# Joining the second half of one mLSTM cell visit with the first half of the next in one block of the schedule

## The chip, the cores and the metric

The kernel runs on one core of a Trainium2 chip. The metric is the device time of one execution in microseconds. Several engines work side by side: TensorE (PE, matrix products; its weight loads are listed as PEld), VectorE (DVE), ScalarE (ACT), GpSimd (POOL) and SyncE (SP), which issues nearly all DMA transfers. Each engine works through its own queue in order; semaphores hold an instruction back until what it reads is there and what it overwrites is no longer needed.

## The reference

Two layers. An mLSTM cell runs over a sequence of 768 tokens for 4 batches and 8 heads of width 40; its output, 3072 tokens by 320, goes through a feed-forward layer of width 2048 with a leaky ReLU.

```python
for t in range(S):                                   # q, k, v, o_gate: (4, 8, 768, 40)
    m_new = np.maximum(f_gate[:, :, t] + m, i_gate[:, :, t])
    f_stab = np.exp(f_gate[:, :, t] + m - m_new)
    i_stab = np.exp(i_gate[:, :, t] - m_new)
    m = m_new
    C = f_stab * C + i_stab * einsum('bhd,bhe->bhde', vt, kt)   # state, 40 x 40 a head
    n = f_stab * n + i_stab * kt
    h_tilde = einsum('bhde,bhe->bhd', C, qt)
    nq = einsum('bhd,bhd->bh', n, qt)
    y[:, :, t] = sigmoid(o_gate[:, :, t]) * h_tilde / np.maximum(np.abs(nq), 1.0)

x = y.transpose(0, 2, 1, 3).reshape(3072, 320)
h = x @ w_in                                          # 320 x 2048
out = np.maximum(0.01 * h, h) @ w_out                 # 2048 x 320
```

## The kernel before

**Steps and groups.** The sequence is cut into 6 chunks of 128 tokens. A *step* `s` is one chunk `c = s // 4` of one batch `b = s % 4`, so there are 24 steps; the state of a batch is carried from step `s - 4` to step `s`. A *group* `g` is the feed-forward work on the four steps of chunk `g`. While PE works on the feed-forward of one group, the cells of later chunks are slipped into its stream. The cells of chunks 2 to 5 (steps 8 to 23) lie in groups 1 to 3.

**Units.** The feed-forward of groups 1 to 3 is cut into 30 units a group, numbered on from 0 to 89. Units 0 to 15 of a group are eight pairs: the first half of a pair opens two PSUM banks `ph` and makes 12 matmuls (line 909), the second half makes 8 more, after which ACT applies the leaky ReLU (line 917) and frees the banks. Units 16 to 29 are the second layer, seven products p1, p2, p6, p7, p4, p5, p3 for two token blocks each (`fast_units`; line 984, 16 matmuls, one bank `po` each). It is a scheme with seven products for eight, whose operands are sums that DVE makes: `mix_early` (line 971, in units 8 and 10 of the group, read by p7), line 1002 (read by p5), line 1007 (in p1 of the second block, read by p6) and line 1019 (in p6, read by p3). The products are taken out of PSUM by ACT for p1, p6, p7 and p4, by DVE for p2, p5 and p3.

**Cells.** A step has two halves on PE. The first half, `u_parts(s)`, makes 16 score products (line 652) and the two state updates dC of the sub-blocks of 64 tokens (line 657) into two banks `sd`; DVE then forms the weights `mixed(s)` (line 662) and adds dC of the first sub-block to the state (`state_add(s, 0)`, line 634). The second half, `u_mix(s)`, multiplies weights and states with the values (`pT`, line 745), forms the next state (`state_next(s, 1)` on POOL, line 630, and `state_add(s, 1)` on DVE, line 634), and lets DVE and POOL turn, gate and scale the result (lines 752 to 763), which goes to DRAM and comes back as `xT` of its group. A *visit* is a pair of steps: 8 visits for 16 steps. `u_mix` of a step comes after its `u_parts`, one to five units later.

**Preparation.** `ready(s)` stands some units ahead of a visit: two DVE transposes of k and q (line 537), the product of q with its decay (line 543), then on POOL the first state product (line 630), the placing of v (line 391), line 510 and the mask (line 482); the exponentials on ACT (line 490) follow three units later, three to a unit (`exps`), and what is left of them runs at the head of `u_parts`. `gates(c)` (DVE scans), `gates_exp(c)` (ACT) and `gates_T(c)` (PE transposes `tg`, DVE copies) make the gates of a chunk. `feed(s)` and `load_late` issue the loads of a step, `spread` and `spread_q` the broadcasts of its decays from the DRAM tensor `a_dr`.

**Buffers.** Two PSUM pools of four banks each: `psf` (tag "mm") holds `ph` and `po`; `psc` (tag "c") holds what belongs to the cells (`sd`, `pT`, `tg`). The bank of dC stays taken until `state_add(s, 1)` in `u_mix`. The tile `w` has 128 x 1024 values a step: its first half is the buffer of the exponentials, its second half first takes v as loaded (320 values).

**Order.** The order on PE, DVE, ACT and POOL is that of the program, written out by hand: `plan[unit]` lists what follows each unit. VISITS says after which units `u_parts` of the eight visits stand, MIXES the same for `u_mix`, READY for `ready` of the next visit's two steps, GATES for `gates` and `gates_exp`, UG for `gates_T`. SP's queue is ordered by the planner of the language.

Of the kernel before, what the change touches and what calls it, by code (L numbers as in the profile page):

```python
# [22 lines left out]
def kernel(  # L23
# [314 lines left out]
            nc.tensor.matmul(t[:], lhsT=ident[:], rhs=ident[:], start=True, stop=True)  # L338

    def gates_T(c, bu):  # L340
        tg = psc.tile([P, 5, BH], F32, name="tg", tag="c")
        kinds = 3 if c == 1 else 2
        for n in range(kinds):
            nc.tensor.transpose(tg[:, n, :], bu[:, n, :], ident[:BH, :BH])
        gT[c] = wk.tile([P, 3, BH], F32, name="gT")
        if c > 0:
            for u in range(2):
                last = SL * (u + 1) - 1
                nc.tensor.matmul(  # L349
                    tg[:, 3 + u, :], lhsT=bu[:, 2, last : last + 1].to_broadcast([BH, P]), rhs=ident[:BH, :BH],  # L350
                    start=True, stop=True,
                )
            gL[c] = f0[:, ts(c % 2, 2 * BH)].rearrange("p (u n) -> p u n", u=2)
        nc.vector.tensor_copy(gT[c][:, :kinds], tg[:, :kinds, :])
        if c > 0:
            nc.vector.tensor_copy(gL[c], tg[:, 3:, :])
# [3 lines left out]
    def load(s):  # L360
        c, b = divmod(s, B)
        rows = ts(c, P)
        d = st.setdefault(s, {})
        n = s % NL
        d.update(k=kn[:, n], q=qn[:, n])
        if c == 0:
            d["va"] = S_t[n][:, 1]
            parts = [(d["k"][:, :, :D], k), (d["q"][:, :, :D], q), (d["va"][:, :, :D], v)]
            for dst, src in parts:
                nc.sync.dma_start(dst, src[b, :, rows, :].rearrange("h p d -> p h d"))  # L370
            return
        nc.sync.dma_start(d["k"][:, :, :D], k[b, :, rows, :].rearrange("h p d -> p h d"))
        w = cw.tile([P, H, P], F32, name="w", bufs=NL)
        flat = w[:].rearrange("p h t -> p (h t)")
        d["w"] = flat[:, : H * SL].rearrange("p (h t) -> p h t", t=SL)
        if c == 1:
            for u in range(2):
                for i in range(2):
                    nc.sync.dma_start(
                        S_v[n][ts(u, SL), u, :, i, :DB],  # L380
                        v[b, :, c * P + u * SL : c * P + (u + 1) * SL, DB * i : DB * (i + 1)].rearrange("h p d -> p h d"),
                    )
            return
        d["vn"] = flat[:, H * SL : H * (SL + D)].rearrange("p (h d) -> p h d", d=D)
        nc.sync.dma_start(d["vn"], v[b, :, rows, :].rearrange("h p d -> p h d"))
# [146 lines left out]
    def prep_kq(s):  # L532

        d = st[s]
        d["kqT"] = cw.tile([P, 2, PR * P], F32, name="kqT")
        for i in range(2):
            nc.vector.transpose(
                d["kqT"][:, i].rearrange("p (h t n) -> p h n t", n=TS, t=QW),
                raw_blocks(s, i, QW).rearrange("p (h n) d -> p h n d", n=TS),
            )  # L540
        for r in range(2):
            rows = ts(r, SL)
            nc.vector.tensor_tensor(  # L543
                mixed(s)[rows, 1 - r], d["kqT"][rows, 1].rearrange("p (h t) -> p h t", t=SL), d["ea"][rows], op=ALU.mult,
            )
# [86 lines left out]
    def state_add(s, u):  # L632
        _, new = state_of(s, 1 - u)
        nc.vector.tensor_tensor(new, new, st[s]["dC", u], op=ALU.add)

    def u_parts(s):
        c, b = divmod(s, B)
        d = st[s]
        kqT, w = d["kqT"], d["w"]
        if c == 1:  # L640
            split_qs(s)
        run(lazy.pop(s))
        bank = [psc.tile([P, H, SL], F32, name=f"sd{r}", tag="c") for r in range(2)]
        ends = 2 if c + 1 < NB else 1
        dC = {}
        for u in range(ends):
            flat = bank[u][SL * u : SL * u + D].rearrange("p h t -> p (h t)")[:, : H * 2 * V1]
            dC[u] = flat.rearrange("p (h k d) -> p h k d", k=2, d=V1)
            d["dC", u] = dC[u]
        for h in range(H):  # L650
            for u, toks, rows in subs(s):
                nc.tensor.matmul(  # L652
                    bank[1 - u][toks, h, :], lhsT=kqT[rows, 0, ts(h, SL)], rhs=kqT[rows, 1, ts(h, SL)], start=True, stop=True,
                )
            for u, toks, rows in subs(s):
                if u < ends:
                    nc.tensor.matmul(  # L657
                        dC[u][:, h].rearrange("p k d -> p (k d)"), lhsT=d["ku"][toks, h],
                        rhs=S_v[s % NL][toks, u, h, :, :V1], start=True, stop=True,
                    )  # L660
        for u, toks, rows in subs(s):
            nc.vector.tensor_tensor(mixed(s)[toks, u], w[toks], bank[1 - u][toks], op=ALU.mult)  # L662
        state_add(s, 0)

    def denominators(den, n):

# [67 lines left out]
    def u_mix(s):  # L734

        c, b = divmod(s, B)
        d = st[s]
        prep_o(s)
        pT = psc.tile([P, PR * P], F32, name="pT", tag="c")
        S, m = S_t[s % NL], mixed(s)  # L740
        for u in range(2):
            for j in range(PR):
                for r in range(2):
                    h = 2 * j + r
                    nc.tensor.matmul(  # L745
                        pT[DP * r : DP * (r + 1), j * P + u * SL : j * P + (u + 1) * SL], lhsT=S[:, u, h, :],
                        rhs=m[:, u, h, :], start=True, stop=True,
                    )
        if c + 1 < NB:
            state_next(s, 1)  # L750
        hb = late_t[:, 2, :].rearrange("p (n d) -> p n d", d=QW)
        nc.vector.transpose(hb.rearrange("p (j n) d -> p j n d", n=TB), in_blocks(pT[:]))
        den = cw.tile([P, PR * TB], F32, name="den")
        denominators(den[:], hb[:, :, DB])
        x3 = xb[:, :, :DB]
        nc.vector.scalar_tensor_tensor(  # L756
            x3, in0=raw_blocks(s, 2, DB), scalar=1.0, in1=hb[:, :, :DB], op0=ALU.add, op1=ALU.mult,
        )
        nc.gpsimd.tensor_tensor(x3, x3, den[:].unsqueeze(2).to_broadcast([P, PR * TB, DB]), op=ALU.mult)  # L759
        if c + 1 < NB:  # L760
            state_add(s, 1)
        xq = cw.tile([P, PR * P], F32, name="x")
        nc.vector.transpose(in_blocks(xq[:]), xb[:].rearrange("p (j n) d -> p j n d", n=TB))  # L763
        nc.sync.dma_start(x_dr[s].rearrange("(j p) t -> p j t", p=P), xq[:].rearrange("p (j t) -> p j t", t=P))
        del st[s]
# [302 lines left out]
    def ahead(s):  # L1068

        if s < NS:  # L1070
# [5 lines left out]
            if s < 2 * B:  # L1076
                prep_qs(s)
            else:
                prep_kq(s)
            if s + NR < NS:  # L1080
                load_late(s + NR, 0)
                load_late(s + NR, 1)
# [74 lines left out]
    with tc.manual_schedule(engines={E.PE, E.DVE, E.Activation, E.Pool}):  # L1157
# [46 lines left out]
                    if s + NL < NS:  # L1204
                        feed(s + NL)

        VISITS = (5, 14, 27, 35, 46, 58, 67, 76)
        MIXES = (7, 17, 29, 37, 51, 60, 69, 77)
        READY = ((7, 8), (18, 25), (32, 33), (41, 42), (51, 54), (62, 66), (69, 72))
        GATES = ((1, 4), (20, 25), (38, 44))  # L1210
        UG = (18, 37, 62)
        PER = NF + 14
        SPLIT = (82, 83, 84, 85, 86, 87, 90, 91, 93, 96, 99, 102)
        plan = collections.defaultdict(list)
# [2 lines left out]
            plan[unit].append((fn, args))  # L1217

        def visit_steps(p):
            return (2 * B + 2 * p, 2 * B + 2 * p + 1) if p < len(VISITS) else ()  # L1220

        def gather():

# [5 lines left out]
            mixed_steps.append(s)  # L1229
            gather()  # L1230

        def load_kq(s):
            load_late(s, 0)
            load_late(s, 1)
            spread_q(s)

        def ready(s):
            late[s] = 3
            lazy[s] = prep_exp(s)
            prep_kq(s)  # L1240
            if s + NR < NS:
                load_kq(s + NR)
            state_next(s, 0)
            place_v(s)
            prep_vu(s)
            prep_mask(s)

        mixed_steps = []
        for p, unit in enumerate(VISITS):
            c = 2 + p // 2  # L1250
            if p % 2 == 0 and c + 1 < NB:
                at_unit(GATES[p // 2][0], gates, c + 1)
                at_unit(GATES[p // 2][1], gates_exp, c + 1)
            for s in visit_steps(p):
                at_unit(unit, u_parts, s)
            for s in visit_steps(p + 2):
                at_unit(unit, feed, s)
            for s in visit_steps(p):
                at_unit(MIXES[p], mix, s)
            for s in visit_steps(p + 1):  # L1260
                at_unit(MIXES[p], load_late, s, 2)
            if p % 2 == 1 and c + 1 < NB:
                at_unit(UG[p // 2], u_gates, c + 1)
            for n, s in enumerate(visit_steps(p + 1)):
                at_unit(READY[p][n], ready, s)

# [14 lines left out]
        for g in range(1, NB):  # L1281
# [3 lines left out]
            for i in range(len(ffs)):  # L1285
# [6 lines left out]
                for fn, args in plan[unit]:  # L1292
                    fn(*args)
                gather()
                if unit == MIXES[-1]:
                    open_parts()
                    for n in range(QN):
                        fetch_w_part(n)
# [36 lines left out]
```

## Time and profile before

| | |
|---|---|
| median of 3 runs | 486.96 us (486.33 to 487.30) |
| profiled execution, own time | 486.61 us |
| profiled execution, span from first to last instruction | 484.5 us |
| granted TensorE clock | 1.000 |
| PE busy | 478.6 us, 99% |
| DVE busy | 364.6 us, 75% |
| ACT busy | 196.1 us, 40% |
| POOL busy | 159.4 us, 33% |

Busy times are sums over instructions; matmuls are pipelined, so a busy PE is not a PE at its peak. Groups 1 to 3 lie between about 131 and 364 us of the span. The chain of work that ended last is followed back from the last instruction; each line of it has the start, the length, and the engine, tile, line and count of a run of instructions. A line of the timeline has the start and length in us, the engine, line, operation, what is written and read, shapes, the count, and in brackets the idle time ahead of it with the instruction that ended it.

### The profile page before, as it was taken

The page shows a single profiled execution, that of the slowest core. Times are in us where ns is not written, and L with a number is a line of the kernel's source. Part 1 is how long each engine was busy: PE and PEld are TensorE (multiplying, and loading weights), DVE is VectorE, ACT ScalarE, POOL GpSimd, SP SyncE. Part 2 cuts the span into 40 slices and gives each one's busy share as a digit, 9 for nine tenths or more (in the row PEclk, how much of TensorE's full clock was granted, in tenths as well). Part 3 has the DMA queues.
Part 4 walks back from the last instruction along what each step waited for, and adds up shares of the span by engine and source line. Part 5 has one row for each costly group of instructions (what it writes and reads, how often), then busy time and mean ns, then how long its engine had stood idle before and what let it go on. Part 6 is the DMA issues. An engine that isn't in the chain of part 4 may idle for free.

```text
span 484.5 us, 12804 instructions
## 1 busy us (share of the span) xinstructions
PE 478.6 (99%) x5113; PEld 371.8 (77%) x5113; DVE 364.6 (75%) x601; ACT 196.1 (40%) x499; POOL 159.4 (33%) x207
## 2 busy tenths in 40 slices
PE   8999999999999999999999999999999999999997
PEld 7998655777645489965569985548998899988996
DVE  4689999889917999777887968689899967335611
ACT  2587864743831331405251121524025642156310
POOL 4128024461601826545451645453210002000020
PEclk9999999999999999999999999999999999999999
DMA  7878778896655677667887867774151030100001
GB/s 144 172 164 195 172 163 169 260 211 146 141 129 111 150 144 212 137 158 194 148 193 171 191 149 177 184 183 123 54 225 40 1 108 1 49 8 0 1 1 54
DMA packets 142698, 63.40 MB, mean 131 GB/s; under 512 B 110832, under 2 KB 130864, under 8 KB 142640
## 3 DMA queue, kind: packets, MB, share of 16 engines
q1 hardware_dynamic: 142256, 62.47, 54.4%
q8 instruction: 40, 0.66, 0.6%
q10 hardware_dynamic: 384, 0.13, 0.1%
q14 instruction: 18, 0.15, 0.1%
HBM read 51.68 MB, written 8.27 MB: 124 GB/s over the span
## 4 chain that ended last, share of the span: by engine, by line
PE 95%; DVE 1%; issue 0%; POOL 0%; POOLq 0%; DVEq 0%
PE po L984 32%; PE ph L909 29%; PE ph L835 8%; PE po L945 7%; PE pe L835 4%; PE pT L745 3%; PE sd L652 3%; PE warm L338 2%; PE pa L675 1%; PE sd L657 1%; PE hN L715 1%; PE tk L566 1%; PE tq L552 1%; PE sc L595 1%; PE tkq L580 0%; PE tg L349 0%
## 5 line engine op out<-in xcount | busy, mean ns | idle before, releaser
L909 PE MATMUL ph<-xT,w_in 64*128 64x512 f32 (+1 forms) x680 | 142.3, 569 | 0.0
L909 PEld LDWEIGHTS ph<-xT,w_in 64*128 64x128 f32 x680 | 64.5, 187 | 66.1 <-issue 63.7
L984 PE MATMUL po<-w_out,acts 128*128 128x160 f32 x640 | 91.0, 301 | 0.0
L984 PEld LDWEIGHTS po<-w_out,acts 128*128 128x128 f32 x640 | 87.5, 190 | 3.4 <-ACT w L490 1.5
L917 ACT ACTIVATE acts<-ph 128x512 f32<-128x512 f32 (+1 forms) x68 | 35.1, 567 | 80.3 <-PE ph L909 80.1
L490 ACT ACTIVATE w<-w,gT 128x64 f32<-128x64 f32 (+1 forms) x192 | 51.8, 348 | 28.1 <-POOL w L482 28.1
L630 POOL TENSOR_TENSOR S<-S,f 40x336 f32<-40x336 f32 x36 | 33.9, 941 | 81.2 <-PE pT L745 47.3
L984 PE MATMUL po<-raw,acts 128*128 128x160 f32 x320 | 45.1, 299 | 0.0
L984 PEld LDWEIGHTS po<-raw,acts 128*128 128x128 f32 x320 | 44.0, 190 | 0.0
L1017 POOL TENSOR_TENSOR y<-y,raw 128x160 f32<-128x160 f32 x10 | 5.5, 556 | 112.2 <-ACT y L1016 112.2
L662 DVE TENSOR_TENSOR qn<-w,sd 64x512 f32<-64x512 f32 x40 | 27.4, 684 | 19.9 <-PE sd L657 11.9
L945 PE MATMUL po<-w_out,acts 128*128 128x320 f32 x128 | 36.6, 437 | 0.0
L482 POOL TENSOR_TENSOR w<-w,i 128x512 f32<-128x512 f32 x20 | 32.4, 1618 | 11.7 <-DMA w<-a_dr 11.7
L857 DVE SCALAR_TENSOR_TENSOR acts<-ph,acts 128x512 f32<-128x512 f32 x32 | 20.6, 685 | 20.6 <-ACT acts L855 20.6
L543 DVE TENSOR_TENSOR qn<-kqT,late 64x512 f32<-64x512 f32 x32 | 33.6, 1049 | 1.0
L945 PEld LDWEIGHTS po<-w_out,acts 128*128 128x128 f32 x128 | 23.6, 190 | 9.1
L759 POOL TENSOR_TENSOR xb<-xb,den 128x320 f32<-128x320 f32 x16 | 11.7, 728 | 48.6 <-DVE xb L756 48.6
L855 ACT ACTIVATE acts<-pe 128x512 f32<-128x512 f32 x32 | 17.4, 595 | 19.0 <-PE pe L835 18.9
L763 DVE STREAM_TRANSPOSE x<-xb 128x512 f32<-128x512 f32 x16 | 17.8, 1109 | 7.8 <-POOL xb L759 7.8
L861 ACT ACTIVATE acts<-acts 128x512 f32<-128x512 f32 x32 | 19.7, 633 | 8.1 <-DVE acts L857 8.1
L984 PE MATMUL po<-raw 128*128 128x160 f32 x160 | 22.7, 300 | 0.0
L652 PEld LDWEIGHTS sd<-kqT 40*64 40x64 f32 x640 | 19.6, 135 | 3.7 <-issue 3.7
(166 smaller groups left out, 786.1 us busy)
## 6 DMA issues: line engine op xcount, KB each, us to landing
w<-a_dr SPq DMA_DIRECT2D x40, 128.0 KB, 3.7
rb<-in_k_dram SPq DMA_DIRECT2D x64, 80.0 KB, 2.8
rb<-in_q_dram SPq DMA_DIRECT2D x64, 80.0 KB, 2.6
rb<-in_o_gate_dram SPq DMA_DIRECT2D x64, 80.0 KB, 2.8
xT<-x_dr SPq DMA_DIRECT2D x32, 160.0 KB, 3.1
late<-a_dr SPq DMA_DIRECT2D x32, 128.0 KB, 3.2
x_dr<-x SPq DMA_DIRECT2D x16, 256.0 KB, 3.0
kn<-in_k_dram SPq DMA_DIRECT2D x24, 160.0 KB, 3.4
```

The source lines that it names most:

```text
L482: nc.gpsimd.tensor_tensor(w, w, cm2.unsqueeze(1).to_broadcast([P, H, SL]), op=ALU.add)
L490: yield nc.scalar.activation(w[:, h, :], w[:, h, :], AF.Exp, bias=gT[c][:, 0, bh : bh + 1], scale=1.0)
L543: nc.vector.tensor_tensor(mixed(s)[rows, 1 - r], d["kqT"][rows, 1].rearrange("p (h t) -> p h t", t=SL), d["ea"][rows], op=ALU.mult,)
L630: nc.gpsimd.tensor_tensor(new, old, g, op=ALU.mult)
L652: nc.tensor.matmul(bank[1 - u][toks, h, :], lhsT=kqT[rows, 0, ts(h, SL)], rhs=kqT[rows, 1, ts(h, SL)], start=True, stop=True,)
L662: nc.vector.tensor_tensor(mixed(s)[toks, u], w[toks], bank[1 - u][toks], op=ALU.mult)
L835: nc.tensor.matmul(ph[r][:], lhsT=parts["w", key][n][part, at : at + P], rhs=xs[key][part, slot, :], start=start and slot == 0, stop=stop ...
L857: nc.vector.scalar_tensor_tensor(fs[r], in0=ph[r][:], scalar=1.0 + EPS, in1=fs[r], op0=ALU.mult, op1=ALU.add,)
L909: nc.tensor.matmul(ph[r][:, cols], lhsT=w_row(r, slot, j), rhs=xT[DP * r : DP * (r + 1), slot, bs, :], start=(slot == 0), stop=(slot == KC ...
L917: nc.scalar.activation(acts[:, f, cols], ph[r][:, cols], AF.Prelu, alpha=0.01)
L945: nc.tensor.matmul(po[n][:], lhsT=acts[:, f, ts(n, P)], rhs=w_out[:, f, :], start=(f == 0), stop=(f == NF - 1),)
L984: nc.tensor.matmul(bank[:], lhsT=left[:, f, :], rhs=right[:, f, :], start=f == 0, stop=f == KH - 1)
```

## The change

Instead of 8 visits and 8 mixes at units of their own, there are nine blocks, BLOCKS. Block `p` holds `u_mix` of visit `p - 1`, then `u_parts` of visit `p`; the first has no `u_mix`, the last no `u_parts`. `gates_T` moves into blocks 1, 3 and 5, at their head.

Because `u_mix` of one visit and `u_parts` of the next stand together, the four banks of `psc` go to `sd` alone: `pT`, and `tg` of chunks 3 to 5, move to `psf`. The bank of dC must be free before the next block: the carried state is therefore formed in `u_parts` already (`carry`: a POOL product and a DVE add) in the second half of the tile `w`, where v is no longer needed, and `u_mix` only copies it into place on POOL. The product of q with its decay moves out of `ready` into the block (`scaled`), since its target is still read by the `u_mix` before; `spread_q` of the next step goes with it. `feed` loads for the next visit, where it loaded for the one after it. READY and GATES have other units.

```diff
     def gates_T(c, bu):
-        tg = psc.tile([P, 5, BH], F32, name="tg", tag="c")
+        pool, tag = (psf, "mm") if c > 2 else (psc, "c")
+        tg = pool.tile([P, 5, BH], F32, name="tg", tag=tag)
...
+    def carried(s):
+        w = st[s]["flat"]
+        rows = state_of(s, 0)[0]
+        return w[rows, H * SL : H * SL + H * 2 * V1].rearrange("p (h k d) -> p h k d", k=2, d=V1)
+
+    def carry(s):
+        c, b = divmod(s, B)
+        rows, old = state_of(s, 1)
+        g = gL[c][rows, 1, ts(b, H)].unsqueeze(2).unsqueeze(3).to_broadcast([D, H, 2, V1])
+        nc.gpsimd.tensor_tensor(carried(s), old, g, op=ALU.mult)
+        nc.vector.tensor_tensor(carried(s), carried(s), st[s]["dC", 1], op=ALU.add)
...
         state_add(s, 0)
+        if 1 < c < NB - 1:
+            carry(s)
...
-        pT = psc.tile([P, PR * P], F32, name="pT", tag="c")
+        pT = psf.tile([P, PR * P], F32, name="pT", tag="mm")
...
         if c + 1 < NB:
-            state_next(s, 1)
+            nc.gpsimd.tensor_copy(state_of(s, 0)[1], carried(s))
...
-        if c + 1 < NB:
-            state_add(s, 1)
...
-        VISITS = (5, 14, 27, 35, 46, 58, 67, 76)
-        MIXES = (7, 17, 29, 37, 51, 60, 69, 77)
-        READY = ((7, 8), (18, 25), (32, 33), (41, 42), (51, 54), (62, 66), (69, 72))
-        GATES = ((1, 4), (20, 25), (38, 44))
-        UG = (18, 37, 62)
+        BLOCKS = (2, 8, 19, 29, 39, 51, 61, 71, 78)
+        READY = ((4, 5), (15, 18), (25, 25), (33, 38), (44, 47), (55, 58), (66, 70))
+        GATES = ((3, 4), (20, 28), (36, 47))
+        UG = (1, 3, 5)
...
         def ready(s):
             late[s] = 3
             lazy[s] = prep_exp(s)
             prep_kq(s)
             if s + NR < NS:
-                load_kq(s + NR)
+                load_late(s + NR, 0)
+                load_late(s + NR, 1)
             state_next(s, 0)
...
+        def scaled(s):
+            q_scaled(s)
+            if s + NR < NS:
+                spread_q(s + NR)
...
+            if p in UG:
+                at_unit(unit, u_gates, 3 + UG.index(p))
+            for s in visit_steps(p - 1):
+                at_unit(unit, mix, s)
+            if p:
+                for s in visit_steps(p):
+                    at_unit(unit, scaled, s)
             for s in visit_steps(p):
                 at_unit(unit, u_parts, s)
-            for s in visit_steps(p + 2):
-                at_unit(unit, feed, s)
+            for s in visit_steps(p + 1):
+                at_unit(unit, feed, s) if p else None
             for s in visit_steps(p):
-                at_unit(MIXES[p], mix, s)
-            for s in visit_steps(p + 1):
-                at_unit(MIXES[p], load_late, s, 2)
-            if p % 2 == 1 and c + 1 < NB:
-                at_unit(UG[p // 2], u_gates, c + 1)
+                at_unit(unit, load_late, s, 2) if p else None
             for n, s in enumerate(visit_steps(p + 1)):
                 at_unit(READY[p][n], ready, s)
```

`q_scaled` is the last loop of the old `prep_kq`, now a function of its own.

More of the change, by code (lines that the diff above doesn't have):

```diff
@@ L373, in load @@
         w = cw.tile([P, H, P], F32, name="w", bufs=NL)
-        flat = w[:].rearrange("p h t -> p (h t)")
+        flat = d["flat"] = w[:].rearrange("p h t -> p (h t)")
         d["w"] = flat[:, : H * SL].rearrange("p (h t) -> p h t", t=SL)
@@ L540, in prep_kq, with q_scaled @@
             )
+    def q_scaled(s):
+        d = st[s]
         for r in range(2):
@@ L1219, in visit_steps @@
         def visit_steps(p):
-            return (2 * B + 2 * p, 2 * B + 2 * p + 1) if p < len(VISITS) else ()
+            return (2 * B + 2 * p, 2 * B + 2 * p + 1) if 0 <= p < len(BLOCKS) - 1 else ()
         def gather():
@@ L1230, in mix @@
             gather()
[L1232 to L1235, printed above, removed]
         def ready(s):
@@ L1246, in ready @@
             prep_mask(s)
+        def scaled(s):
+            q_scaled(s)
+            if s + NR < NS:
+                spread_q(s + NR)
         mixed_steps = []
-        for p, unit in enumerate(VISITS):
+        for p, unit in enumerate(BLOCKS):
             c = 2 + p // 2
@@ L1294 @@
                 gather()
-                if unit == MIXES[-1]:
+                if unit == BLOCKS[-1]:
                     open_parts()
```

## The prediction

> **What bounds the kernel now.** I read the page first (parts 1 and 4), then the chain of waits in order of time, then the timelines of VectorE (DVE) and GpSimd (POOL).
>
> ```profile
> PE 478.6 (99%) x5113; PEld 371.8 (77%) x5113; DVE 364.6 (75%) x601; ACT 196.1 (40%) x499; POOL 159.4 (33%) x207
> ...
> PEclk9999999999999999999999999999999999999999
> ...
> PE 95%; DVE 1%; issue 0%; POOL 0%; POOLq 0%; DVEq 0%
> ```
>
> TensorE (PE) is busy for 99% of the span at full clock and is 95% of the chain; from 43 us on the list of waits gives it no wait at all. So time can be won only by shortening PE's own stream, and is lost by any wait put into it. The chain shows what the stream pays where it changes its kind of matmul (start, length, count):
>
> ```profile
> 46.03 1.03 PE tk L566 x64
> ...
> 64.89 1.06 PE hN L715 x32
> 65.95 1.03 PE tk L566 x64
> ...
> 115.34 1.06 PE hN L715 x32
> ...
> 145.93 4.49 PE ph L909 x20
> 150.42 2.02 PE pT L745 x64
> 152.44 15.65 PE ph L909 x72
> ...
> 178.57 2.37 PE po L984 x16
> ...
> 181.63 19.76 PE po L984 x144
> ...
> 229.54 2.02 PE pT L745 x64
> 231.55 0.24 PE tg L344 x2
> ```
>
> Two stretches of ph: (15.65 - 4.49) / (72 - 20) = 0.2146 us a matmul, so 20 of them are 4.29 and the stretch has 0.20 us besides. Two of po: (19.76 - 2.37) / 128 = 0.1359, and 2.37 - 16 x 0.1359 = 0.20 again. Every uninterrupted stretch of feed-forward matmuls thus carries a fixed 0.197 us. A small cell's stretch has a fixed part too, but keeps it whatever stands next to it: pT is 2.02 ahead of ph and ahead of tg, hN 1.06 ahead of tk and of po, tk 1.03 behind ph and behind hN.
>
> **The change, part by part.** PE: before, 16 cell stretches and two tg apart from them (units 18 and 62) break the feed-forward stream 18 times; after, 9 blocks do. 9 x 0.197 = **1.77 us less**. Order inside a block is tg, pT, pT, sd, sd. The trace has no pT followed by sd. Bounds: hN (128*64 tiles) followed by tk (64*40) keeps both at full length, saving nothing more; tq followed by sd at 52.4, both on 64-row tiles, runs on without a break, which would save sd's fixed part of 0.15 (2.01 less 32 groups of 0.058) in 7 blocks, 1.0 more. pT uses 128*64 tiles and sd 40*64 and 64*40, as hN and tk do, so I take nothing. The Trainium skill's page TensorEngine Tiling (Array Packing), Key Properties, says that a change of tiling mode drains the engine; by that rule too the sum stays at 1.77, and the trace agrees where shapes change (0.2 us).
>
> DVE, the engine that PE will wait for. Its timeline at one mix, and one ready step where POOL works beside it:
>
> ```profile
> 151.55 0.72 DVE L752 STREAM_TRANSPOSE late<-pT 128x512 f32<-128x512 f32 x1 [2.63 <-PE pT L745]
> ...
> 153.00 0.49 DVE L756 SCALAR_TENSOR_TENSOR xb<-rb,late 128x320 f32<-128x320 f32 x1
> 153.53 0.51 DVE L634 TENSOR_TENSOR S<-S,sd 40x336 f32<-40x336 f32 x1
> 154.40 1.10 DVE L763 STREAM_TRANSPOSE x<-xb 128x512 f32<-128x512 f32 x1 [0.36 <-POOL xb L759]
> 155.53 0.72 DVE L752 STREAM_TRANSPOSE late<-pT 128x512 f32<-128x512 f32 x1
> ```
>
> The state_add that leaves u_mix (0.51) lay beside POOL's product L759 (153.64 to 154.37), for which L763 waits anyhow: removing it gains nothing. carry() puts its like into u_parts, where nothing covers it: POOL starts 0.15 after its releaser, as L759 does after 153.49; its product costs 0.76 (L630 alone); DVE starts 0.03 later; then the add, 0.50. That is **1.44 us of DVE time a step**, for 12 steps, queued ahead of the next u_parts, mix_early (L971), the ready steps' transposes and the sums L1002 to L1019 that PE reads. POOL's state_next(s,1), 0.76, becomes a copy, 0.45 (L391): off the path. The moved q_scaled (L543, two a step) costs 0.69 each alone (187.89) and 1.05 on average beside POOL's mask; in the block POOL is mostly idle, so I take 0.72. One block on DVE: 2 x 3.98 (mix, 151.55 to 155.53) + 4 x 0.72 + 2 x (1.84 + 1.44) (145.17 to 147.01 for u_parts) = **17.4 us**, or 18.7 with 1.05.
>
> Where PE meets that, from a block's first pT (whose end lets DVE start at 1.1; 2.02 + 2.01 of cells on PE):
> - Block 8, banks: all pT now share psf with ph, which holds two banks there. Unit 10 comes at 0.68 (tg) + 4.03 + 0.2 + 1.72 = 6.6; the second pT's bank is free at 0.68 + 1.1 + 3.98 + 0.75 = 6.5. Slack 0.1; cost 0 to 0.5.
> - End of group 1: p3's second half (unit 29) needs the second L1019. PE is there at 4.2 + 9 x 2.17 = 23.7. DVE: 1.1 + 17.4 + 1.14 + gates(4) + 1.14; gates takes 1.7 alone (133.18) and 3.3 beside POOL (191.04), I take 2.5 as POOL has ready(14) in hand by then: 23.3, no wait. Block 29 opens with tg, which now needs a psf bank, and all four hold p5 and p3 results that DVE releases behind two pairs of transposes (2.6) and 0.5 of adds: 26.4 against PE's 25.9. Wait **0.5**, between 0 and 1.4.
> - Group 2: p6 at unit 50 needs the first L1007. PE is there at 4.2 + 12.9 (three pairs) + 8.7 = 25.8 after block 39; DVE at 1.1 + 17.4 + 1.2 + 1.3 + 3 x 1.14 = 24.4. Slack 1.4; in the run shown it is 1.3 (L1007 done 259.2, p6 at 260.5).
>
> SP's queue: spread_q now waits for q_scaled, at 1.1 + 8 + 2.9 = 12 us into a block, and the next steps' k, v and w are issued behind it; they land 3.4 to 3.8 us later (part 6), about 16.5, and POOL asks for them behind the second carry, at 18. Slack 1.5; if it goes, exponentials and then the activations L917 behind them on ACT are late next. Block 78 for mix 77: its DVE work began 2 us after pT ended anyway (339.90), cost 0; the split for group 4 has 0.5 us of slack (done 364.6, used 365.2).
>
> Sum on the profiled execution: 486.61 own time, 484.5 span, 2.1 around it. Span 484.5 - 1.77 + 0.5 = 483.2; own time 485.3. The median shown is 0.35 above that execution, so **485.7 us**.
>
> **Rivals.**
> *DVE becomes the bound (slower).* In the window 150.35 to 260.50 (group 1's pair 4 to group 2's p6) PE is busy 110.15 of 110.15, DVE 94.45, and DVE's eight waits inside mixes, 0.37 each, take 3.0: 12.7 us are free. Eight steps' carries fill 11.5 of them. What tips it is POOL's ready work falling on the big sums:
>
> ```profile
> 160.91 1.71 POOL L482 TENSOR_TENSOR w<-w,i 128x512 f32<-128x512 f32 x1
> 162.70 1.10 POOL L630 TENSOR_TENSOR S<-S,f 40x336 f32<-40x336 f32 x1
> ...
> 163.20 1.68 DVE L971 TENSOR_TENSOR raw<-acts 128x1024 f32<-128x1024 f32 x1
> ```
>
> L971 takes 1.68 here and 1.22 alone; ready(12), (13), (18) and (19) now sit where L1002 and L1007 are queued. With 1.6 for each sum, 3.3 for gates and 18.7 a block: unit 29 waits 2.6, tg 0.9, p6 1.7, block 8 0.5, in all 5.7, so +3.9; halfway between that and the forecast it is +1.8. It decides once the waits pass 1.77, about 0.8 us more DVE time per block than I take. Time 487.9 to 490.9. For it: the 1.2 us left over. Against: L543 itself no longer meets the mask. The Trainium skill's SBUF — State Buffer, Who interferes with whom, says that a DVE instruction with two SBUF inputs and a reading POOL instruction exclude one another, the later one blocked outright; the trace agrees in kind (0.69 becomes 1.65 at 161.52).
> *The waits eat the saving.* The same places at 0.8 to 2.7 in all: 486.0 to 487.9.
> *No drain between pT and sd.* Another 1.0 less: 484.7, or 484.2 without waits. Against it stands hN with tk.
>
> **How the numbers follow.** 0.2% of 487, about 1.0 us, is what a measurement here can tell from no change. Forecast (waits under 0.8) 0.42 and no drain 0.05 are faster: 0.47. Eaten saving 0.20 is same. DVE-bound 0.33 is slower; SP's lateness would act through the same waits and is in it. The forecast's own range is 485.2 (no wait) to 486.0. The whole range runs from no drain, 484.3, to 489.5, past the middle of the slow rival, leaving out about 0.13.
>
> **What would show it.** Right: nine cell stretches in the chain, pT 2.02 followed by sd 2.01, ph stretches still n x 0.2146 + 0.2, PE waits under 0.8 in sum, the first at tg L344 of unit 29. On DVE a gap of 0.9 ahead of each of 12 adds by carry, L543 near 0.7. Wrong: PE waiting for L1007, L1019 or a bank held by L752 for over 1 us each; sd shorter behind pT; PE waits on ACT L917 behind exponentials; DVE gaps that end on a_dr loads.

## The result: 4.5 us slower, and the profile after

The median after is 491.19 us (490.92 to 492.49, 4 runs), before 486.72 (486.33 to 487.30, 4 runs of the same session): ratio 1.0094, 95% interval 1.0081 to 1.0107. The forecast was 485.7. The profiled execution after has a span of 489.1 us, 484.5 before.

The page of the changed kernel, parts 1 and 4:

```profile
PE 479.2 (98%) x5113; PEld 373.8 (76%) x5113; DVE 362.1 (74%) x601; ACT 196.9 (40%) x499; POOL 164.0 (34%) x219
...
PE 80%; DVE 6%; SPq 4%; DMA 3%; issue 2%; POOL 1%; ACT 0%; DVEq 0%; POOLq 0%; ACTq 0%
```

PE was 95% of the chain and is 80%: the chain now runs through DVE, through loads and through "issue", which means that an engine stood still and waited for nothing the profile records. PE's list of waits (line waited for, us, times, longest) names where:

```profile
PE sd L675 <- issue: 1.3, 2, 0.8
PE sd L670 <- issue: 1.1, 1, 1.1
PE pT L765 <- DVE f L357: 1.0, 1, 1.0
PE ph L927 <- ACT acts L935: 0.8, 1, 0.8
PE po L1002 <- DVE acts L1025: 0.5, 1, 0.5
```

(Lines after: ph 927, relu 935, po 1002, pT 765, sd 670 and 675, sums 1020, 1025, 1037, q_scaled 547, weights of `u_parts` 680, the carry 651 on POOL and 652 on DVE, `mix_early` 989, the mask 483.)

The list counts from the end of a matmul, and the profile only models that end. I use starts instead: a stretch of n matmuls is priced as in the prediction (ph n x 0.2146 + 0.197, po n x 0.1359 + 0.197, pT 2.015, sd 2.011), and what it takes beyond that is lost. Before, every stretch of groups 1 to 3 has its price. After, seven do not:

| block or unit | what stands still | us lost |
|---|---|---|
| unit 8 | ph, for the relu L935 | 1.50 |
| block 19 | in the middle of sd | 0.97 |
| block 29 | in the middle of sd | 0.78 |
| block 39 | at the end of sd | 0.05 |
| unit 50 (p6) | po, for the sum L1025 | 0.78 |
| block 51 | second pT, for tg's bank | 1.22 |
| block 51 | in the middle of sd | 1.29 |

That is 3.10 in sd and 3.50 elsewhere. From the first ph of group 1 to the last matmul of the kernel it is 349.81 us before and 354.60 after, +4.79; nine interruptions fewer are -1.77, and -1.77 + 6.60 = +4.83. So the saving came, and 6.6 us of waits were put against it. The other 0.3 lie ahead of group 1 (its first ph at 131.07 instead of 130.77), in a part whose program the change leaves as it was; the end behind the last matmul is 0.4 shorter.

**How the carry reaches PE.** DVE's timeline after block 2, where gates of chunk 3 now stand behind the two carries:

```profile
140.84 0.50 DVE L638 TENSOR_TENSOR S<-S,sd 40x336 f32<-40x336 f32 x1
142.27 0.51 DVE L652 TENSOR_TENSOR w<-w,sd 40x336 f32<-40x336 f32 x1 [0.94 <-POOL w L651]
...
145.56 0.51 DVE L652 TENSOR_TENSOR w<-w,sd 40x336 f32<-40x336 f32 x1 [0.87 <-POOL w L651]
146.08 0.56 DVE L295 TENSOR_TENSOR_SCAN F<-fi,zeros 32x128 f32<-32x128 f32 x1
...
148.27 1.35 DVE L305 TENSOR_TENSOR bu<-il,F 32x128 f32<-32x128 f32 x1
```

and the chain behind it:

```profile
149.68 0.66 DVE na L315
...
150.37 0.35 ACT bu L326
150.72 0.13 ACT bu L327
...
150.86 0.58 ACT acts L935
...
151.49 0.69 PE ph L927
```

Each carry costs 0.94 or 0.87 of waiting and 0.51 of adding. The gates start only at 146.08; two of their small instructions take 1.35 and 0.72 while POOL has a mask and a state product in hand; the gates' exponentials on ACT end at 150.95; the relu stands behind them, and PE behind the relu.

The second place is group 2. DVE's timeline, then POOL's beside it:

```profile
256.10 1.36 DVE L989 TENSOR_TENSOR raw<-acts 128x1024 f32<-128x1024 f32 x1
257.38 1.29 DVE L538 STREAM_TRANSPOSE kqT<-rb 128x512 f32<-128x512 f32 x2
258.60 2.90 DVE L1020 TENSOR_TENSOR acts<-acts 128x1024 f32<-128x1024 f32 x2
261.43 4.00 DVE L1025 TENSOR_TENSOR acts<-acts 128x1024 f32<-128x1024 f32 x2
```

```profile
260.39 2.24 POOL L483 TENSOR_TENSOR w<-w,i 128x512 f32<-128x512 f32 x1
262.71 1.63 POOL L634 TENSOR_TENSOR S<-S,f 40x336 f32<-40x336 f32 x1
264.39 1.84 POOL L392 COPY S<-w 64x320 f32<-64x320 f32 x2
```

Both sides stretch: the sums take 1.2 to 2.3 each (1.2 alone), the mask 2.24 (1.28 in the median). p6 waits for the first L1025, and the sums that follow carry the lateness into block 51 (chain; start, us, what):

```profile
267.22 3.58 DVE acts L1037 x2
270.80 0.13 DVE gT L355
270.94 0.14 DVE f L357
271.08 0.14 issue
271.22 1.15 PE pT L765 x32
...
273.80 0.22 PE sd L670 x7
274.02 1.06 issue
275.09 0.21 PE sd L670
```

The last three lines are the other kind: PE is in the middle of its 128 sd matmuls, past every semaphore that it has to pass (they stand at the first matmuls of a step), and stops for 1.06 us. Part 3 of the page has the candidate:

```profile
q8 instruction: 40, 0.66, 0.5%
```

40 transfers of 16 KB, one in 256 of PE's 10,226 weight loads and matmuls. The trace has the times of each: 

```
pause in sd        last 16 KB transfer   landed to resumption
186.42 .. 187.39   184.99 .. 185.86      1.53
214.38 .. 215.16   212.78 .. 213.72      1.43
273.80 .. 275.09   272.51 .. 273.58      1.51
```

The Trainium skill, Trainium Architecture — The Big Picture, section The software stack, says that an instruction has 64 bytes, which makes 16 KB 256 of them, and that the streams are put into the engines' instruction memory when the program is loaded. The first agrees with the trace (one transfer in 256); for the second the transfers run all through this execution.

### The profile page after: what moved, and what is told of

The parts are those of the page before. It is cut to its first block, busy times and chain, and to the rows that moved or that the text cites. A ratio compares the mean times of both kernels' runs of the same rounds, so it can differ in the third digit from the quotient of the medians.

```text
span 489.1 us, 12792 instructions
## 1 busy us (share of the span) xinstructions
PE 479.2 (98%) x5113; PEld 373.8 (76%) x5113; DVE 362.1 (74%) x601; ACT 196.9 (40%) x499; POOL 164.0 (34%) x219
## 4 chain that ended last, share of the span: by engine, by line
PE 80%; DVE 6%; SPq 4%; DMA 3%; issue 2%; POOL 1%; ACT 0%; DVEq 0%; POOLq 0%; ACTq 0%
PE po L1002 29%; PE ph L927 19%; PE ph L853 8%; PE po L963 7%; PE pe L853 4%; PE pT L765 3%; PE sd L670 2%; PE warm L338 2%; SPq L443 2%; DMA rb<-in_q_dram 1%; PE pa L695 1%; DVE qn L547 1%; DMA rb<-in_o_gate_dram 1%; SPq L430 1%; PE hN L735 1%
## 5 line engine op out<-in xcount | busy, mean ns | idle before, releaser
L1002 PE MATMUL po<-w_out,acts 128*128 128x160 f32 x640 | 89.4, 300 | 0.0
L935 ACT ACTIVATE acts<-ph 128x512 f32<-128x512 f32 (+1 forms) x68 | 34.9, 566 | 72.8 <-PE ph L927 72.5
L1035 POOL TENSOR_TENSOR y<-y,raw 128x160 f32<-128x160 f32 x10 | 9.0, 909 | 98.0 <-ACT y L1034 97.9
L875 DVE SCALAR_TENSOR_TENSOR acts<-ph,acts 128x512 f32<-128x512 f32 x32 | 20.6, 685 | 21.2 <-ACT acts L873 21.1
L680 DVE TENSOR_TENSOR qn<-w,sd 64x512 f32<-64x512 f32 x40 | 27.4, 685 | 8.4 <-PE sd L675 5.9
L634 POOL TENSOR_TENSOR S<-S,f 40x336 f32<-40x336 f32 x24 | 23.6, 984 | 29.3 <-PE hN L735 18.9
L483 POOL TENSOR_TENSOR w<-w,i 128x512 f32<-128x512 f32 x20 | 28.8, 1438 | 10.8 <-ACT acts L935 10.8
L651 POOL TENSOR_TENSOR w<-S,f 40x336 f32<-40x336 f32 x12 | 9.1, 760 | 55.0 <-DVE S L638 55.0
L873 ACT ACTIVATE acts<-pe 128x512 f32<-128x512 f32 x32 | 17.4, 595 | 22.6 <-PE pe L853 22.6
L392 POOL COPY S<-w 64x320 f32<-64x320 f32 x32 | 21.1, 660 | 13.0 <-DMA w<-in_v_dram 11.6
L547 DVE TENSOR_TENSOR qn<-kqT,late 64x512 f32<-64x512 f32 x32 | 22.3, 698 | 0.7
L670 PE MATMUL sd<-kqT 40*64 40x64 f32 x640 | 21.8, 220 | 1.1 <-issue 1.1
```

The source lines that it names most:

```text
L392: nc.gpsimd.tensor_copy(S_v[s % NL][toks, u, :, :, :DB], st[s]["vn"][toks].rearrange("p h (k d) -> p h k d", d=DB),)
L483: nc.gpsimd.tensor_tensor(w, w, cm2.unsqueeze(1).to_broadcast([P, H, SL]), op=ALU.add)
L547: nc.vector.tensor_tensor(mixed(s)[rows, 1 - r], d["kqT"][rows, 1].rearrange("p (h t) -> p h t", t=SL), d["ea"][rows], op=ALU.mult,)
L634: nc.gpsimd.tensor_tensor(new, old, g, op=ALU.mult)
L670: nc.tensor.matmul(bank[1 - u][toks, h, :], lhsT=kqT[rows, 0, ts(h, SL)], rhs=kqT[rows, 1, ts(h, SL)], start=True, stop=True,)
L935: nc.scalar.activation(acts[:, f, cols], ph[r][:, cols], AF.Prelu, alpha=0.01)
```

## The experiments

Medians and ratios are from all runs of a kernel, the other figures from its one profile. The median of the kernel before lay between 486.72 and 486.92 from round to round, and each ratio is to the one of its own round. "Stretch" runs from the first ph of group 1 to the last matmul; "in sd" and "elsewhere" are what its parts take beyond their price.

| run | median us | ratio to before, 95% | stretch | in sd | elsewhere |
|---|---|---|---|---|---|
| before | 486.8 | | 349.81 | 0 | 0 |
| after | 491.19 | 1.0081 to 1.0107 | 354.60 | 3.10 | 3.50 |
| e1_pad | 498.05 | 1.0209 to 1.0267 | 354.26 | 2.02 | 4.23 |
| e2_noadd | 487.74 | 1.0009 to 1.0029 | 351.04 | 3.03 | 0 |
| e3_gates | 491.67 | 1.0062 to 1.0116 | 355.75 | 4.69 | 1.37 |
| e4_tg | 490.87 | 1.0045 to 1.0089 | 353.88 | 3.02 | 2.84 |
| e5_addfirst | 487.12 | 0.9999 to 1.0025 | 351.14 | 3.12 | 0 |
| e6_split | 490.93 | 1.0069 to 1.0095 | 354.24 | 0.45 | 4.75 |
| e7_both | 485.80 | 0.9971 to 0.9991 | 350.25 | 1.22 | 0 |
| e8_carry_alone | 489.98 | 1.0048 to 1.0077 | 353.61 | 0 | 3.81 |
| e9_sd_later | 485.52 | 0.9968 to 0.9988 | 348.80 | 0 | 0 |
| e10_carry_first | 486.19 | 0.9977 to 0.9995 | 349.81 | 0 | 0 |
| e11_split4 | 485.72 | 0.9968 to 0.9986 | 350.45 | 0 | 1.05 |

Each stretch is 349.81, less 1.77 for the kernels with nine blocks, plus the two columns and the price of parting a block again (e6, e7: 3 x 0.344; e9: 4 x 0.197; e11: 4 x 0.344), to within 0.05; e3 has 1.67 more, told below. Since a column is what a part takes beyond its price, this sum tests the prices and the 1.77, best in the rows whose columns are 0.

**e1: is it the supply of instructions?** The stops stand at the same place modulo 256 of PE's instructions, so 72 more instructions at the start must move them.

```diff
+    def pad(n):
+        t = psf.tile([P, P], F32, name="warm", tag="mm")
+        for _ in range(n):
+            nc.tensor.matmul(t[:, :1], lhsT=ident[:], rhs=ident[:, :1], start=True, stop=True)
...
-warm 3; warm 4; g 0; ld 0; ld 1; ge 0; lo 0; lo 1
+pad 18; warm 3; warm 4; g 0; ld 0; ld 1; ge 0; lo 0; lo 1
```

> Edit: 18 one-column matmuls ahead of the first warm-up matmul, which put 72 instructions (36 passes, each a weight load and a matmul) into PE's stream at the very start and change nothing else. Theory A: the three pauses in the middle of sd (0.97, 0.78 and 1.29 us in blocks 19, 29 and 51) are PE running out of instructions. In the trace of the changed kernel PE's 16 KB instruction transfers come once in 256 of its instructions, each pause ends 1.4 to 1.5 us after one has landed, and each stands at the same place modulo 256. Counted so, 72 instructions more move those places out of the blocks 19 and 51 and to the edge of block 29 (0 to 0.5 us left), and one into block 8 (0.8 to 1.4). Sum of pauses in sd 0.8 to 2.3 instead of 3.0; time 489.0 to 490.5. Theory B: sd waits for a PSUM bank, for GpSimd's vu or for VectorE; then the pauses stay in blocks 19, 29 and 51 with their sizes, none comes in block 8, and the time stays at 491.2 within 0.5.

The chain in block 8, which had no stop before, and the end of pT and sd in block 19, which had one (two windows of one view):

```profile
166.31 0.11 PE sd L675 x4
166.42 1.12 issue
167.54 0.24 PE sd L675 x2
...
191.55 2.02 PE pT L770 x64
...
195.47 0.11 PE sd L675 x4
195.58 2.51 PE po L1007 x17
```

In block 8 sd now loses 1.33, in block 19 nothing, in block 51 nothing, in block 29 still 0.69, which is 0.2 more than I allowed it. Theory B, under which nothing should move, is out. The forecast of the total was wrong: the 36 passes took 0.213 us each at that place, as long as passes with 128 columns there, and the first ph of group 1 came 7.0 us later than in the run after. In the stretch 1.08 less in sd brought only 0.34: p6 now waited 1.83. So the stops moved to where instruction supply puts them, and yet taking some of them away alone gained nearly nothing.

**e2: is the carry on DVE the cause of the rest?**

```diff
         nc.gpsimd.tensor_tensor(carried(s), old, g, op=ALU.mult)
-        nc.vector.tensor_tensor(carried(s), carried(s), st[s]["dC", 1], op=ALU.add)
```

> Edit: the carry keeps GpSimd's product but leaves out VectorE's addition (so the state handed on lacks it), which frees 1.44 us of VectorE a step (0.94 of waiting, 0.50 of adding), 12 times. Theory A (VectorE's queue, lengthened by the carries, sets the waits outside sd): the waits at ph L927 near 150 (1.3 to 1.5), at po L1002 near 263 (0.78) and at pT L765 near 270 (1.22) fall under 0.3 each, 2.5 to 3.3 in all, while the pauses in sd stay between 2 and 4 in sum: time 487.9 to 488.9. Theory B (these waits come from GpSimd's work beside the sums and from ScalarE's order; the carries are covered): each stays above 0.6, time 490.5 to 491.5. Theory C (the carries cause the pauses in sd as well): all go, 484.9.

Every wait outside sd is gone and the stops in sd are as large as they were: theory A in both halves, 0.2 below its range. Theories B and C are out.

**e3 and e4: can the waits be taken away one by one?** One edit moves the gates' exponentials of chunk 3 from unit 4 to unit 6, the other gives tg its old bank.

```diff
-        GATES = ((3, 4), (20, 28), (36, 47))
+        GATES = ((3, 6), (20, 28), (36, 47))
```

> Edit: the exponentials of chunk 3's gates are queued on ScalarE at unit 6 instead of unit 4, so that the activations L935 of unit 5 no longer stand behind them. Theory A: the wait of 1.3 to 1.5 us at unit 8 is only this order on ScalarE; it goes and nothing takes its place, 489.8 within 0.4. Theory B: VectorE is behind by then anyway (gates of chunk 3 and sums behind the carries), and the time comes back as a wait of about the same size at the next sums or at tg of block 8: 491.2 within 0.5.

```diff
-        pool, tag = (psf, "mm") if c > 2 else (psc, "c")
+        pool, tag = psc, "c"
```

> Edit: tg takes its bank from psc again, as before the change. Theory A: the wait of 1.22 us of the second pT in block 51 is for the bank that tg holds until VectorE copies it; it goes, 490.0 within 0.4. Theory B: the bank that the second pT then takes is held by a sum that VectorE reaches at the same time (L1037 ends 270.8, the copy 271.07), so only 0.2 to 0.4 of it goes: 490.9 within 0.4.

In each the wait aimed at is gone (unit 8: 1.50 to 0; pT of block 51: 1.22 to 0). In e3 the wait for p6 rose from 0.78 to 0.96, that of pT fell to 0.41, and the stop in block 51 grew to 2.53, behind a transfer that began only with the stop (272.26; the stop from 272.27). Behind it the granted clock was half for 3.4 us, which is the 1.67; whether the stop brought that on is not shown. In e4 the p6 wait rose to 1.30, so 0.66 of the waits was gained. Its first ph came at 134.01, 2.9 later than after, and the times are spread from 489.13 to 493.16, those of e3 from 488.89 to 493.47. Both medians lie in theory B's range, but with this spread the totals decide little; the profile of e4 speaks for part of the time coming back.

**e5: the same instructions, the wait covered.** `u_parts` does `state_add`, then POOL's product, then the two weights L680, then the carry's addition (`carry` is now the product alone, `carry_add` the addition).

```diff
-        for u, toks, rows in subs(s):
-            nc.vector.tensor_tensor(mixed(s)[toks, u], w[toks], bank[1 - u][toks], op=ALU.mult)
-        state_add(s, 0)
-        if 1 < c < NB - 1:
-            carry(s)
+        if 1 < c < NB - 1:
+            state_add(s, 0)
+            carry(s)
+        for u, toks, rows in subs(s):
+            nc.vector.tensor_tensor(mixed(s)[toks, u], w[toks], bank[1 - u][toks], op=ALU.mult)
+        if 1 < c < NB - 1:
+            carry_add(s)
+        else:
+            state_add(s, 0)
```

> Edit: in u_parts VectorE adds the first half's state and GpSimd forms the carry's product ahead of the two products L680, and VectorE's addition of the carry comes behind them; the same instructions in another order, so that the two L680 (1.37 us) cover GpSimd's product (0.15 + 0.76). Theory A: of the carry's 1.44 us a step the 0.94 of waiting goes; with 1.44 gone (the run without the addition) no wait outside sd was left, so those at 150, 263 and 270 (1.5, 0.8, 1.2) fall to under 0.4 each; the pauses in sd (about 3.0) stay: 487.6 to 488.9. Theory B: GpSimd's product slows the two L680 beside it (0.69 to 0.9 or more) and the 0.50 of the additions is enough to keep half of the waits: 489.3 to 490.6.

487.12, 0.5 below theory A's range. DVE's timeline in block 8 (the weights stand at line 686 here, the addition at 655):

```profile
165.77 0.50 DVE L638 TENSOR_TENSOR S<-S,sd 40x336 f32<-40x336 f32 x1
166.19 1.39 DVE L686 TENSOR_TENSOR qn<-w,sd 64x512 f32<-64x512 f32 x2
167.51 0.50 DVE L655 TENSOR_TENSOR w<-w,sd 40x336 f32<-40x336 f32 x1
```

No gap is left ahead of the addition, and the weights beside POOL's product take 1.39 for two as they did alone. That is the rule of the Trainium skill, SBUF — State Buffer, Who interferes with whom, from its other side: a DVE instruction with one input in SBUF does not contend with POOL. These have their second input in PSUM; the sums, with both inputs in SBUF, are the ones that stretched. PE's waits from 43 us on:

```profile
PE sd L673 <- issue: 1.3, 1, 1.3
PE sd L678 <- issue: 1.1, 2, 0.6
```

So 0.94 us of DVE's waiting a step, not its work, was what made PE wait outside sd.

**e6, e7: the stops taken away, alone and with e5.** The second sd of three blocks goes behind the next unit.

```diff
-            for s in visit_steps(p):
-                at_unit(unit, u_parts, s)
+            for n, s in enumerate(visit_steps(p)):
+                at_unit(unit + (n if p in (2, 3, 5) else 0), u_parts, s)
```

> Edit: in blocks 19, 29 and 51 the sd of the second step moves behind the next feed-forward unit, so that no stretch of cell matmuls there is longer than pT and one sd (258 PE instructions where it was 386). Theory A (instruction supply): the three pauses in sd go (3.0), three more interruptions cost 0.2 each (0.6), the waits outside sd keep their sizes within 0.5: 488.8 within 0.6. Theory B (VectorE is the bound by now, and PE only meets it elsewhere): what sd gives up comes back at po L1002 and pT L765, 490.4 to 491.5.

> Both edits: the addition first, and the second sd of blocks 19, 29 and 51 one unit later. Theory A (two causes that add: 3.0 of instruction supply, 3.5 of VectorE's waiting for the carry's product): only the merging's saving of 1.77 less 0.6 for three more interruptions, and waits under 0.8 in sum, are left: 485.4 to 486.8, that is 0 to 1.5 faster than before. Theory B (the causes are one and the same time, or VectorE binds as soon as sd no longer pauses): 487.5 to 489.

e6 takes the stops out of its three blocks (0.45 is left, in block 39, whose transfer came later than in the run after), and the time stays: 490.93. The waits elsewhere went from 3.50 to 4.75, and parting three blocks cost 1.03 (0.344 each, an interruption and sd's fixed part; I had written 0.2). The time is theory B's: with the waiting in the carry, DVE sets the pace, and what a stop of PE gives up comes back as a wait. That the carry brought all of it back is not shown: 0.91 of the 4.75 is a wait that the run after does not have. Behind block 29 PE waited for the bank of the second pT, because DVE had stood still for 3.44 us ahead of L776; the view names a load, but ACT's work on the same tile (L527) ended just then, at 217.07 (L776 starts at 217.10).

With the waiting covered (e7) the same edit brings 1.3 more by the medians, 0.89 in the stretch, and the median is 0.1 to 0.3% below that of before. The profiled run of e7 (486.82 us) is one of its slowest: it has a stop of 1.22 in block 39, and its stretch is still 0.44 longer than before. The median lies in theory A's range, but that range asks only that both causes be gone. Taken away singly they do not add up: e5 alone -4.07, e6 alone -0.26, both -5.39 (in the stretch -3.46, -0.36 and -4.35).

**e8, e10: the carry in the old order.** The kernel before with the carry alone, first as the change has it, then with the addition behind the weights as in e5.

```diff
+        if 1 < c < NB - 1:
+            carry(s)
...
-            state_next(s, 1)
+            nc.gpsimd.tensor_copy(state_of(s, 0)[1], carried(s))
...
-        if c + 1 < NB:
-            state_add(s, 1)
```

> Edit: the kernel before with the carry alone: the carried state formed in u_parts and copied in u_mix; visits and mixes where they were, sixteen interruptions, q_scaled in the ready steps. Theory A: with pT and sd apart VectorE has room for 1.44 us a step between them, so that the carry costs little, and no pause in sd comes (its 256 instructions stand alone): 486.7 to 487.9. Theory B: VectorE's time is the bound wherever the carry stands (12 steps of 1.44, 12.7 us free in groups 1 and 2): waits of 1.5 to 4 before L1002 and tg, 488.5 to 491.

> Edit: the kernel before with the carry alone (sixteen visits and mixes as they were), now with the addition of the first half and GpSimd's product ahead of the two products in u_parts. The carry alone with the waiting in it gave 489.98. Theory A: the 0.94 of waiting a step was what it cost, the 0.50 of adding fits into what VectorE has free: 486.6 to 487.4. Theory B: the additions alone are too much as well: 488.2 or more.

The chain of e8 ahead of p6 of group 2:

```profile
261.89 0.51 DVE w L648
262.40 0.03 issue
262.43 1.23 DVE acts L1016
263.66 1.15 DVE acts L1021
264.80 0.14 issue
264.94 1.19 PE po L998 x7
```

The carry's addition, the two sums, PE: with no block merged and sums at full speed the carry costs 3.2 us (3.81 in the stretch), theory B. With the wait covered it costs nothing (the stretch is 349.81 again), theory A. e10's median lies 0.4 below theory A's range and 0.6 below before's. Its profiled span is 0.6 shorter as well, and none of that is in the stretch: 0.44 lies behind the last matmul, where the run before took 3.60 and all other profiles about 3.16, and 0.16 ahead of group 1. Why the end was longer there is open.

**e9, e11: no stops, no waits.** Both with e5; e9 moves both sd of blocks 19, 29, 39 and 51 one unit later, e11 only the second.

```diff
-                at_unit(unit, u_parts, s)
+                at_unit(unit + (p in (2, 3, 4, 5)), u_parts, s)
```

> Edit: the addition first, and both sd of blocks 19, 29, 39 and 51 one unit later than the block's pT, so that pT (130 PE instructions) and sd (256) are parted by a feed-forward unit in every block in which a boundary between instruction transfers falls into pT. Theory A: no pause in sd is left (the last one stood in block 39, 1.2 us), four more interruptions cost 0.2 each and sd keeps one fixed part: 1.77 less 0.79 below before, 484.9 to 486.0. Theory B: sd four us later leaves VectorE idle ahead of it and short of time behind it: waits at po L1002 or pT of over 0.8, 486.3 or more.

> Edit: as in the run with both edits, and the second sd of block 39 one unit later too. Theory A: the pause of 1.2 us in block 39 goes for 0.34 (an interruption and a fixed part of sd): 485.0 to 485.6, and the spread of the runs is smaller, as no run meets a pause any more. Theory B (a wait on VectorE in block 39 comes in its place): 485.8 or more.

e9's list of PE's waits holds nothing behind the warm-up matmuls of the start, and its chain is again PE's:

```profile
PE 95%; DVE 1%; issue 0%; POOL 0%; POOLq 0%; DVEq 0%
```

Its stretch is 348.80, 1.01 below before, where 1.77 - 0.79 = 0.98 was worked out; 485.52 us, in theory A's range, is the best median of all, 0.12 to 0.32% below before by the interval. e11 has no stop either, but its median of 485.72 lies between the two ranges: its second pT of block 51 waited 0.97 for tg's bank; its times are spread over 1.1 us, e7's over 2.3 (484.81 to 487.15).

In the eight profiles that have them there are 19 stops in sd of over 0.4 us, and each ends 1.31 to 1.63 us after a 16 KB transfer has landed, 2.3 to 2.8 after it began. Counted in order of start, from 0, with PE's semaphore instructions and drains (10,335 in all in the run after), every one of the 19 stands ahead of an instruction whose number is 193 modulo 256. Take the first transfer for the second such place, the next for the third and so on: in none of the thirteen profiles does PE pass a place less than 1.31 us after its transfer has landed. The speed of the 256 instructions between two places does not decide alone, for the kernel before ran them as fast three times without a stop. It is also when the transfer begins, told here from the moment at which PE passes the place before:

```
run, place passed   the 256 took, less the stop   transfer began   stop
before 143.89       2.50                          4.41 ahead       none
before 251.00       2.65                          3.60 ahead       none
before 281.23       2.88                          2.29 ahead       none
after  183.82       2.60                          1.17 behind      0.97
after  212.08       2.31                          0.70 behind      0.78
after  237.44       2.83                          0.09 ahead       0.05
after  271.30       2.51                          1.21 behind      1.29
```

In the three rows of before PE was still in feed-forward matmuls when the transfer began (9 to 15 instructions a us by their prices, where sd has 127), 33 to 42 instructions short of the place.

## Why the prediction was wrong

**PE's saving: right.** Nine interruptions fewer, 1.77, with the prices accounts for every stretch of the table to 0.05 us; e9, which waits nowhere, shows it best (348.80, where 348.83 was to come).

**pT ahead of sd: right.** pT 2.015, then sd 2.011 where nothing stops it. The rule of the Trainium skill, TensorEngine Tiling (Array Packing), Key Properties, a drain at a change of mode, agrees with both, and the rival "no drain" is out.

**The sizes on DVE: right in the main.** L547 0.698 on average (0.72 taken), the carry 0.94 or 0.87 + 0.51 (1.44 taken), a block 16.9 to 17.2 in four cases (17.4 taken). Block 29 took 19.3: one small instruction beside POOL's mask 1.21 instead of 0.19, and a wait of 0.92 for ACT.

**The waits, 0.5 in the sum: the step that failed.** The one that the sum had, at tg of block 29, did not come; others measured 6.60, in two parts.

- 3.50 by DVE, the rival "DVE becomes the bound", whose price of 5.7 less 1.77 gave +3.9 (its halfway value, written as +1.8, comes to +1.3 from its own figures). I gave it 0.33. Of its four places one was right: p6 with 1.7 priced and 0.78 found. There the slack of 1.4 went because DVE started 0.6 late on a ready step's transposes and because the run from L989 to the first L1025 took 7.6 instead of 5.9: the sums cost what the rival said (1.6), not what the forecast took (1.14). Unit 29 (2.6) and tg of block 29 (0.9) did not wait. Unit 8 (1.50) and block 51 (1.22) were not in the list; I had looked at block 8 for a bank only, and not at what the gates behind the first two carries do to ACT's order. My own count, 11.5 us of carries into 12.7 us free, said that DVE would be full; I should have let that decide. I also took the 1.44 as given, where another order of the same instructions makes it 0.50 (e5).
- 3.10 in sd, for which no rival stood. I priced the joined stretch by the kinds of matmul in it and not by their number: pT and sd together are 386 instructions in 4.03 us, and one of the places above, met in the first 130 of them, leaves 256 to run in 2.1 to 2.9 us (64 of pT's or 127 of sd's a us) while their transfer has only just begun, or has not begun yet. Before, sd stood alone behind feed-forward matmuls; where 256 ran that fast, their transfer had begun 2.3 to 4.4 us ahead.

**SP's queue: right in part.** No gap of DVE ended on a load of a_dr. But in block 39 v landed 20.6 us behind the first pT (16.5 taken), so that the slack was gone and POOL waited 1.46 for it; in e5 and e9 POOL waited 2.7 and 2.6 at the same place and PE did not wait, so this lateness alone cost nothing there. **Block 78: right,** nothing was lost behind block 71. **Block 8's bank: right,** no wait.

## What to carry to other kernels

When a cross-engine product feeds an addition, put independent work of the adding engine between them before anything else is judged: here 0.9 us of waiting twelve times cost 3.8 us (e8 against e10) and 4.1 us (after against e5), and the reordering cost nothing. When fast matmuls are joined into one run, count instructions as well as time, and compare the run with what one instruction transfer holds, and with what stands ahead of it while that transfer is fetched. Take two suspected causes away alone and together: a stop of the engine that is ahead can cost next to nothing until the engine behind it has been mended.

## What was not expected of the hardware

PE can run out of instructions: its stream comes in 16 KB transfers (40 in this kernel), and where 256 instructions ran in 2.1 to 2.9 us and their transfer began late, it stood still for 0.4 to 1.5 us, once for 2.5, until 1.31 to 1.63 us after the transfer had landed. The place goes by the instruction count modulo 256 (193 in all 19 cases), so 72 instructions at the start moved stops that lie 150 us later. In the first 9 us of e1 a matmul pass with one column took 0.213 us, as one with 128 columns did behind it. The first ph of group 1 came between 130.5 and 134.0 us in these profiles, in the twelve kernels that have the same work ahead of it; in the latest of them hN waited 1.5 us for DVE, and why is open.
